# Transposing q and k as 32-bit words that hold two tokens, with kept-back MoE matmuls and a moved lead-in, in an attention and MoE kernel

## The chip, the cores and the metric

The kernel runs on one core of one Trainium2 chip. The metric is the device time of one execution in microseconds (us). Each run carries a state, fast or slow, and only fast runs are compared. The engines are TensorE (PE; its weight loads, which overlap it, are listed as PEld: 270.1 and 141.1 us busy in the kernel before, in a span of 294.5), VectorE (DVE), ScalarE (ACT) and GpSimd (POOL).

## The reference

Causal attention by blocks of 64 tokens over 8 batches of 8 heads, 576 tokens of 64 values, then a mixture layer of two first matmuls, a maximum and an output matmul:

```python
scores = (q @ k.transpose(0, 1, 3, 2)) / np.sqrt(64)      # q, k, v: 8 x 8 x 576 x 64, float32
scores = np.where(block_i >= block_j, scores, -1e9)       # blocks of 64
attn = softmax(scores)
x = (attn @ v).transpose(0, 2, 1, 3).reshape(4608, 512)
out = np.maximum(x @ w1, x @ w2) @ w_out                  # w1, w2: 512 x 1024; w_out: 1024 x 512
```

## The kernel before

The heads go in 32 pairs. A group of two pairs of q (or k) is loaded, cast to bf16 and transposed on PE. For every pair the scores come in two bursts (`burst_a`, `burst_b`) whose exponentials run on ACT; two pairs later the product with v (`av`) is formed in two parts, normalised by DVE (`rec`, `xp`) and transposed into xT (`x_out`). Between these pieces `fill(n)` issues n of the MoE matmuls that are ready: `h` (x times w1 and w2) and `y` (times w_out). Eight of them make a unit.

```python
def cast(nm, g, parts):
    t = raws.pop((nm, g)).rearrange("p s (t d) -> p t s d", d=D)
    qk_n[nm, g] = n = qkn.tile([P, RPP, 2, D], BF16, name=f"{nm}n")        # RPP = 9
    for copy, j0, j1 in parts:
        copy(out=n[:, j0:j1], in_=t[:, j0:j1])

def transposes(nm, g, copies):
    n = qk_n.pop((nm, g))
    pts = [ps_m.tile([P, RPP, NP], BF16, name=f"ps_{nm}T", tag="m") for _ in range(2)]
    for j in range(RPP):
        for i in range(2):                                                 # partitions 0-63, 64-127
            r = slice(i * NP, (i + 1) * NP)
            nc.tensor.transpose(pts[i][:, j, :], n[r, j].rearrange("p s d -> p (s d)"), ident[r, r])
    ...     # DVE or ACT copy pts[i] to qT / kT: out "q (p j) -> q p j", in "q j p -> q p j"

def av(p, ts):
    po = ps_m.tile([P, n, 2, D + 1], FP32, name="ps_o", tag="m")           # the same four buffers
    ...     # 6 matmuls for ts = [0, 1], 24 for [2, 3, 4]; then rec and xp read po

def fill_of(s):
    ...     # 27 for the last two pairs
    left = 10 - s if s < 10 else 4 - (s - 2) % 4
    return -(-ready() // left)
```

The softmax here doesn't subtract the row's maximum and nothing guards it: scores larger than these inputs give would overflow.

## Time and profile before

The three runs before the change have a median of 296.89 us. The run that was profiled took 296.26 us, a span of 294.5. PE is the bound, with 92% busy and 82% of the chain: the prediction below shows its lines. I use one derived figure, the *lag*: the time at which a pair's first score matmul starts, less 0.216 us (the start-to-start time of a settled MoE matmul) for every MoE matmul issued before it. What the lag grows by in a stretch is time that PE gave to anything but MoE matmuls, work or waiting. It is worked out from the instruction records.

| what, kernel before | value |
|---|---|
| lag at the first scores of pair 0 | 8.35 us |
| growth to pair 2, to pair 4 | 7.73, 14.71 |
| growth from pair 4 to 10 (h and y run between, waits for casts) | 15.49 |
| growth 10 to 16, 16 to 28, 28 to 31 | 16.22, 29.99, 7.22 |
| the tail behind pair 31 | 6.39 |
| settled transposes of one group, start to start | 0.27 us |

The rest of the time is the MoE matmuls themselves at 0.216 us each.

### The profile page before, as it was taken

Reading aid. Unit: us, or ns where it says so; the run is one execution under the profiler, and the core shown is the slowest. Engines: PE = TensorE matmul, PEld = TensorE weight load, DVE = VectorE, ACT = ScalarE, POOL = GpSimd, SP = SyncE. Lnnn points to the kernel's source line nnn. Section 1 sums busy time; section 2 is a strip of 40 time slices with the busy share of each in tenths; the row PEclk is TensorE's granted clock in tenths of the full one; section 3 lists DMA queues with packets and bytes.
Section 4 is the critical chain, followed back from the end, with each engine's and each line's share of the span. In section 5 each row is a group of like instructions: output and inputs, shape, how many; then the busy total and the mean of one; then the engine's idle time right before and its main releaser. Section 6 shows DMA issues by size and latency. Waiting matters only on the chain.

```text
span 294.5 us, 7341 instructions
## 1 busy us (share of the span) xinstructions
PE 270.1 (92%) x3033; PEld 141.1 (48%) x3080; DVE 182.6 (62%) x362; ACT 138.4 (47%) x200; POOL 94.4 (32%) x214
## 2 busy tenths in 40 slices
PE   1677989899998999999999999999999999999995
PEld 1245434554554555555554555555544554444443
DVE  6546657647877676666676666667655776464530
ACT  3865557685664555555555555555544000100112
POOL 3955166544632443244324432244210000000000
PEclk9999999999999999999999999999999999999999
DMA  7999997997970639455924792566201011110114
GB/s 270 140 250 314 294 175 119 68 270 247 323 46 2 71 98 183 128 125 103 195 68 168 78 225 41 171 71 75 47 36 44 33 47 60 38 71 36 71 38 143
DMA packets 56082, 36.65 MB, mean 124 GB/s; under 512 B 38769, under 2 KB 43377, under 8 KB 56049
## 3 DMA queue, kind: packets, MB, share of 16 engines
q0 software_dynamic: 41728, 7.87, 33.3%
q1 hardware_dynamic: 13760, 27.60, 27.3%
q10 hardware_dynamic: 560, 0.72, 0.7%
q8 instruction: 24, 0.39, 0.6%
q14 instruction: 10, 0.07, 0.1%
HBM read 34.60 MB, written 9.44 MB: 150 GB/s over the span
## 4 chain that ended last, share of the span: by engine, by line
PE 82%; DVE 8%; ACT 5%; issue 2%; DMA 2%; POOL 1%; POOLq 0%; ACTq 0%; DVEq 0%
PE ps_h L166 41%; PE ps_y L184 19%; PE ps_o L325 10%; PE ps_s L274 7%; ACT aT L280 4%; DVE g L175 2%; PE ps_kT L257 2%; DMA qraw<-in_q_dram 2%; PE ps_qT L257 2%; DVE kT L264 1%; DVE xp L332 1%; PE ps_xe L345 1%; DVE xT L350 1%; DVE xT L351 1%; PE ps_y L201 1%
## 5 line engine op out<-in xcount | busy, mean ns | idle before, releaser
L280 ACT ACTIVATE aT<-ps_s 128x1024 bf16<-128x1024 f32 (+1 forms) x128 | 99.3, 832 | 84.5 <-PE ps_s L274 82.2
L166 PE MATMUL ps_h<-xT,w_sb 128*128 128x512 bf16 x543 | 133.4, 380 | 4.3 <-DVE xT L351 2.6
L166 PEld LDWEIGHTS <-w_sb 128*128 128x128 bf16 x576 | 51.8, 98 | 61.9 <-issue 9.2
L173 DVE CAST h<-ps_h 128x512 bf16<-128x512 f32 x72 | 49.7, 690 | 36.7 <-PE ps_h L166 33.6
L184 PE MATMUL ps_y<-wo_sb,g 128*128 128x512 bf16 x266 | 66.6, 379 | 1.1 <-DVE kT L264 0.3
L285 POOL MEMSET aT<- 64x128 bf16 x128 | 23.4, 201 | 118.2 <-ACT aT L280 118.0
L175 DVE TENSOR_TENSOR g<-h,ps_h 128x512 bf16<-128x512 bf16 x72 | 49.5, 688 | 13.2 <-PE ps_h L166 12.4
L190 ACT COPY y<-ps_y 128x512 f32<-128x512 f32 x35 | 20.6, 588 | 56.9 <-PE ps_y L184 43.7
L325 PE MATMUL ps_o<-vv,aT 128*128 128x65 bf16 x960 | 40.5, 196 | 2.1 <-DVE kT L264 0.6
L325 PEld LDWEIGHTS <-aT 128*128 128x128 bf16 x960 | 35.8, 99 | 13.3 <-issue 3.2
L274 PE MATMUL ps_s<-qT,kT 64*128 64x64 bf16 (+4 forms) x384 | 36.7, 291 | 4.9 <-ACT aT L280 3.3
L184 PEld LDWEIGHTS <-g 128*128 128x128 bf16 x280 | 25.6, 98 | 27.3 <-issue 0.4
L109 POOL DMA_DIRECT2D vv<-in_v_dram x40 | 33.7, 849 | 2.2 <-DMA w_sb<-in_moe_w_dram 2.2
L332 DVE TENSOR_TENSOR xp<-ps_o,rec 128x256 bf16<-128x256 f32 x64 | 31.4, 491 | 2.2
L331 DVE RECIPROCAL rec<-ps_o 128x4 f32<-128x4 f32 x64 | 11.8, 185 | 26.9 <-PE ps_o L325 26.7
L274 PEld LDWEIGHTS <-kT 64*128 64x128 bf16 x384 | 16.9, 97 | 20.6 <-issue 13.7
L264 DVE COPY kT<-ps_kT 128x576 bf16<-128x576 bf16 x17 | 12.8, 756 | 10.4 <-PE ps_kT L257 10.4
L105 POOL CAST qn<-qraw 128x1152 bf16<-128x1152 f32 (+1 forms) x15 | 17.0, 1132 | 5.3 <-DMA qraw<-in_q_dram 4.5
L264 DVE COPY qT<-ps_qT 128x576 bf16<-128x576 bf16 x17 | 12.8, 756 | 7.8 <-PE ps_qT L257 7.7
L105 POOL CAST kn<-kraw 128x1152 bf16<-128x1152 f32 x13 | 14.9, 1147 | 0.8
L257 PE MATMUL ps_qT<-ident,qn 64*128 64x64 bf16 x288 | 7.5, 197 | 6.6 <-DVE qn L105 6.4
L264 ACT COPY qT<-ps_qT 128x576 bf16<-128x576 bf16 x15 | 9.5, 630 | 4.9 <-PE ps_qT L257 4.9
(36 smaller groups left out, 89.7 us busy)
## 6 DMA issues: line engine op xcount, KB each, us to landing
qraw<-in_q_dram SPq DMA_DIRECT2D x16, 576.0 KB, 5.4
out_dram<-y SPq DMA_DIRECT2D x35, 256.0 KB, 2.0
kraw<-in_k_dram SPq DMA_DIRECT2D x15, 576.0 KB, 6.9
vv<-in_v_dram POOLq DMA_DIRECT2D x32, 128.0 KB, 4.5
w_sb<-in_moe_w_dram POOLq DMA_DIRECT2D x4, 256.0 KB, 14.2
w_sb<-in_moe_w_dram POOLq DMA_DIRECT2D x2, 512.0 KB, 23.3
wo_sb<-in_moe_w_out_dram POOLq DMA_DIRECT2D x2, 512.0 KB, 12.6
kraw<-in_k_dram ACTq DMA_DIRECT2D x1, 576.0 KB, 5.4
```

What stands on the lines that cost most here:

```text
L105: copy(out=n[:, j0:j1], in_=t[:, j0:j1])
L109: nc.gpsimd.dma_start(out=vv_r[b % NV][:rows, c, :, :D], in_=v[b, :, c * P:c * P + rows, :].rearrange("h p d -> p h d"),)
L166: nc.tensor.matmul(pt[:], w_sb[:, c, f * P:(f + 1) * P], xT[:, c, t0:t0 + SPAN], start=(c == 0), stop=(c == NDM - 1),)
L173: nc.vector.tensor_copy(out=h1[:], in_=pt[:])
L175: nc.vector.tensor_max(g[:, f, :], h1[:], pt[:])
L184: nc.tensor.matmul(py[:], g[:, f, s * P:(s + 1) * P], wo_sb[:, f, :], start=(f == 0), stop=(f == NFF - 1),)
L264: copies[i](out=t[:, :S].rearrange("q (p j) -> q p j", j=RPP), in_=pts[i].rearrange("q j p -> q p j"),)
L274: nc.tensor.matmul(ps[:m, hh, col:col + w], kT[r, c * P:c * P + m], qT[r, q0:q0 + w], start=True, stop=True,)
L280: nc.scalar.activation(out=aT_r[p % NA][:m, :, a0:a0 + w], in_=ps[:m, :, :w], func=AF.Exp, scale=scale,)
L285: nc.gpsimd.memset(aT_r[p % NA][BLK:, :, a0:a0 + BLK], 0.0)
L325: nc.tensor.matmul(po[:, gi, hh, :], a[:, hh, a0:a0 + P], vv[:, c, h0 + 2 * hh, :], start=(mm == 0), stop=(mm == n_mm - 1),)
L332: nc.vector.tensor_mul(xp[:, ts[0]:ts[0] + n, :, p % 2], po[:, :, :, :D], rec[:, :n].to_broadcast([P, n, 2, D]),)
```

## The change

Its intent is fewer, denser transposes. Two neighbouring tokens' bf16 values are cast side by side into one 32-bit word; the word is transposed as fp32; each PSUM row then holds adjacent bf16 tokens, so the copy out of PSUM reads unit steps. Nine rows are odd, so a tenth, padded one is added. Further: at most all but six of the ready MoE matmuls are spread, so that six are left to cover the wait for xT (`KEEP`); the casts of q and k group 3 go from POOL to DVE and ACT; and in the first four pairs the transposes of k1 and the AV matmuls move.

```diff
-        qk_n[nm, g] = n = qkn.tile([P, RPP, 2, D], BF16, name=f"{nm}n")
+        qk_n[nm, g] = n = qkn.tile([P, RPP // 2 + 1, 2, D, 2], BF16, name=f"{nm}n")
+        to = n.rearrange("p j s d e -> p e j s d")
         for copy, j0, j1 in parts:
-            copy(out=n[:, j0:j1], in_=t[:, j0:j1])
+            for e in range(2):
+                a, z = (j0 - e + 1) // 2, (j1 - e + 1) // 2
+                copy(out=to[:, e, a:z], in_=t[:, 2 * a + e:2 * z + e - 1:2])
...                                     # memsets of the padding for the first six tiles; ident32
-        pts = [ps_m.tile([P, RPP, NP], BF16, ...) for _ in range(2)]
+        pts = [ps_m.tile([P, NP, nj], FP32, ...) for _ in range(2)]        # nj = 5
...
-                    pts[i][:, j, :], n[r, j].rearrange("p s d -> p (s d)"), ident[r, r],
+                    pts[i][:, :, j], n[r, j].rearrange("p s d e -> p (s d e)").bitcast(FP32),
+                    ident32[r, r],
...                                     # the copy out reads the words as bf16 pairs, 9 of 10
+    KEEP = 6
-        return -(-ready() // left)
+        return -(-max(0, ready() - KEEP) // left)
...
-            cast("q", 3, ((pool, 0, RPP),))       # in pool_work(3), behind DMA issues
-            cast("k", 3, ((pool, 0, RPP),))
...
         burst_a(s)                                # pairs 0 to 3
         if s == 0:
             cast("k", 1, ((dve, 0, RPP),))
-        if s >= 2:
-            av(s - 2, [0, 1])
+        elif s == 1:
+            transposes("k", 1, (dve, dve))()
+        elif s == 2:
+            av(0, [0, 1])
+        else:
+            av(0, [2, 3, 4])
         burst_b(s)
...                                     # av(1) follows pair 3, together with av(2) and av(3)
         burst_a(s)                                # pairs 4 to 31
+        if s == HP + 1:
+            cast("q", 3, ((dve, 0, RPP),))
+            cast("k", 3, ((act, 0, RPP),))
```

More of the change, by code (lines that the diff above doesn't have):

```diff
@@ L82 @@
     ident = wpool.tile([P, P], BF16, name="ident")
+    ident32 = wpool.tile([P, P], FP32, name="ident32")
     raws = {}
@@ L102, in cast @@
         t = raws.pop((nm, g)).rearrange("p s (t d) -> p t s d", d=D)
-        qk_n[nm, g] = n = qkn.tile([P, RPP, 2, D], BF16, name=f"{nm}n")
+        qk_n[nm, g] = n = qkn.tile([P, RPP // 2 + 1, 2, D, 2], BF16, name=f"{nm}n")
+        to = n.rearrange("p j s d e -> p e j s d")
         for copy, j0, j1 in parts:
-            copy(out=n[:, j0:j1], in_=t[:, j0:j1])
+            for e in range(2):
+                a, z = (j0 - e + 1) // 2, (j1 - e + 1) // 2
+                copy(out=to[:, e, a:z], in_=t[:, 2 * a + e:2 * z + e - 1:2])
+        if (nm, g) in (("q", 0), ("q", 1), ("q", 2), ("k", 0), ("k", 1), ("k", 2)):
+            nc.vector.memset(n[:, RPP // 2, :, :, 1], 0.0)
     def load_v(b, c):
@@ L133 @@
     make_identity(nc, ident)
+    make_identity(nc, ident32)
     for r in range(NV):
@@ L252, in transposes @@
         n = qk_n.pop((nm, g))
-        pts = [ps_m.tile([P, RPP, NP], BF16, name=f"ps_{nm}T", tag="m") for _ in range(2)]
-        for j in range(RPP):
+        nj = RPP // 2 + 1
+        pts = [ps_m.tile([P, NP, nj], FP32, name=f"ps_{nm}T", tag="m") for _ in range(2)]
+        for j in range(nj):
             for i in range(2):
@@ L265, in copy_out @@
                     out=t[:, :S].rearrange("q (p j) -> q p j", j=RPP),
-                    in_=pts[i].rearrange("q j p -> q p j"),
+                    in_=pts[i].rearrange("q p j -> q (p j)").bitcast(BF16).rearrange(
+                        "q (p j) -> q p j", j=2 * nj)[:, :, :RPP],
                 )
@@ L415 @@
             cast("k", 1, ((dve, 0, RPP),))
-        if s >= 2:
-            av(s - 2, [0, 1])
+        elif s == 1:
[4 more added lines that the diff above has]
+            av(0, [2, 3, 4])
         burst_b(s)
         pool_work(s)
-        if s < 2:
-            transposes("qk"[s], 1, (dve, dve))()
-        else:
-            av(s - 2, [2, 3, 4])
-    for p in (2, 3):
+        if s == 0:
+            transposes("q", 1, (dve, dve))()
+    for p in (1, 2, 3):
         av(p, [0, 1])
         av(p, [2, 3, 4])
-        x_out(p - 2)
+        if p == 2:
+            x_out(0)
+    x_out(1)
     x_due = []
```

## The prediction

> **What bounds the kernel now.** I read the page first, then the groups by shape, the waits of TensorE (PE), the timeline of a settled stretch, and the chain of waits in the first 45 us. Busy time and chain:
>
> ```profile
> PE 270.1 (92%) x3033; PEld 141.1 (48%) x3080; DVE 182.6 (62%) x362; ACT 138.4 (47%) x200; POOL 94.4 (32%) x214
> PE 82%; DVE 8%; ACT 5%; issue 2%; DMA 2%; POOL 1%; POOLq 0%; ACTq 0%; DVEq 0%
> ```
>
> PE is busy 92% of the span and carries 82% of the chain; nobody else is near. The idle 24 us (294.5 - 270.1) lie early: by stretches, PE is busy 16.3 of the first 29 us, 33.1 of 29 to 66, and 126.0 of the 129 us from 91 to 220. What it waits for from 66 to 220 us is short:
>
> ```profile
> PE ps_h L166 <- DVE xT L351: 2.0, 5, 0.6
> PE ps_o L325 <- DVE kT L264: 0.6, 2, 0.3
> PE ps_o L325 <- DVE qT L264: 0.3, 1, 0.3
> ```
>
> The 2.0 us are the five moments when a batch's last x transpose has just been issued and no older MoE matmul is left to run while DVE copies xT.
>
> The transposes concerned, settled (start, duration, engine, operation):
>
> ```profile
> 102.98 0.44 PE L257 MATMUL ps_kT<-ident,kn 64*128 64x64 bf16 x18
> 103.25 0.41 PE L274 MATMUL ps_s<-qT,kT 64*128 64x320 bf16 x6
> ```
>
> Start to start, a group of 18 takes 103.25 - 102.98 = 0.27 us, not the 0.44 that its overlapping records span: 15 ns each, because the two halves (partitions 0-63, 64-127) run side by side. There are 32 groups, so q and k transposes cost PE only 32 x 0.27 = 8.6 us, about 3% of the span. That caps what part one can save.
>
> The evacuation copies, by shape:
>
> ```profile
> L264 DVE COPY qT<-ps_qT 128x576 bf16<-128x576 bf16 x17 | 12.8, 756 | 7.8 <-PE ps_qT L257 7.7
> L350 DVE COPY xT<-ps_xe 128x640 bf16<-128x640 bf16 x16 | 7.8, 486 | 2.6 <-PE ps_xe L345 2.5
> ```
>
> 576 elements read with a step cost 756 ns; 640 read in unit steps, also from PSUM, cost 486.
>
> The early stretch: group 3's casts stand on POOL behind DMA issues that wait, and PE waits for them:
>
> ```profile
> 39.16 1.14 POOL qn L105
> 40.31 1.10 POOL kn L105
> 41.41 0.05 issue
> 41.45 0.62 PE ps_kT L257 x17
> 42.07 0.02 issue
> 42.09 0.77 DVE kT L264
> 42.86 0.04 issue
> 42.90 1.46 PE ps_h L166 x6
> ```
>
> The last h matmul before this stretch has streamed by about 40.0 (it starts at 39.8), the next starts at 42.9; useful PE work between is two transpose groups and six scores, 0.27 + 0.27 + 0.35 = 0.9 us, so 2.0 us are lost.
>
> [...] No fp32 transpose is in this trace. [...] The trace records 98 ns per bf16 load but starts one every 15 ns, so the recorded duration is no pitch; what an fp32 pitch is stays open, and is the largest uncertainty here.[...]
>
> **The change, part by part.** On the instruction lists 576 bf16 transposes (18 a group, each with its own weight load) become 320 fp32 ones (10 a group, no separate weight load listed). Everything else on PE has the same counts.
>
> *Transposes.* A group changes from 0.27 us to t. If an fp32 pair (both halves) streams as one bf16 pair does, t = 10 x 15 ns = 0.15 us: -0.12 x 32 = -3.8 us.[...] The first eight groups (0 to 3) lie where PE waits for other things, so 24 groups count in full: -2.9[...] us. I take 0.30 us[...]: +0.03 x 24 = +0.7 us. I choose nearer the fast end because six padding memsets, a larger tile and retuning were spent around this trick, which only makes sense if it did not cost 20 us; that is an inference about the author and not from the profile.
>
> *Copies.* Source rows become 9 adjacent values of 10[...], what the 640-element xT copy needs: about 490 ns in place of 756. 34 DVE copies save 34 x 0.27 = 9 us of DVE, but DVE is 62% busy: on the path only the 0.9 us of ps_o waits and a few tenths early; -0.5 us. ACT's 627 ns copy[...] I leave it.
>
> *Casts.* One of 1152 becomes 640 + 512 with an output step of two. POOL pays one more fixed cost per cast (estimate: the 1152 cast takes 1149 ns, a 384 one 891 beside DVE; some 0.2 us), about 25 x 0.2 = 5 us on an engine that is 32% busy: off the path. At the very start it adds perhaps 0.2 us before the first scores, with the memsets.
>
> *Moved casts q3, k3* to DVE and ACT: the 2.0 us of waiting above go.
>
> *Moved AV and k1 transpose, first four pairs.* In the chain exp gives way to PE from 14.5 to 16.7 (k1 transpose and its copy) and from 18.7 to 21.0 (24 AV matmuls between score bursts). Moving k1 between the bursts and pushing AV back saves about 0.9 + 1.0 us of that; the DVE normalisations overlap better. My sum is a first h matmul near 26.3 in place of 29.4.
>
> *But the weights.* The six w_sb transfers land at 22.0, 25.2, 29.6, 34.1, 38.1 and 40.6 us (issue time plus time to landing in the DMA view; the last is 16.4 + 24.2), with DMA at 0.9 or more of its time through that stretch. Each h unit of 8 matmuls needs both w halves: h matmul 21 needs the one at 34.1, 33 the one at 38.1, 37 the one at 40.6. Walking the new order (6, q2/k2, 6, scores, 7, scores, 8, scores, 6, q3/k3, scores, 7) from 26.3, matmul 21 would be up at about 33.0 and waits 1.1 us; 37 is up at 40.1 and waits 0.5; matmul 40 ends near 41.5. In the kernel before matmul 41 ends at about 44.3, 40 at 44.1. So the AV part and the cast part, worth 3.1 + 2.0 singly, together give some 2.5 us; the rest becomes a wait for weights.
>
> *Kept-back MoE (six matmuls, 1.3 us)* cover the wait for xT, at most 0.6 us each: -2.0 us from 66 to 220, none from work, as the kept ones are only done later.
>
> Sum: -2.5 - 2.0 - 0.5 + 0.2 + 0.7 = -4.1, on 296.89: 292.8; with the transposes' skew to the fast end I say 292.3.
>
> **Rivals.** *Fp32 weight loads become the bound*[...]. For it: [...]PE has no slack to hide it. Against: row halves overlap in this trace, and weight loads run ahead. *Transposes at 15 ns each and DMA less strict*: -2.9 in place of +0.7 and 1 us more early: 288 us. For it: transfers may also start earlier as buffers come free sooner. Against: DMA is full until 40 us whatever the order. *Early gains hidden wholly by weights or by v of batch 1* (lands by 45.9, while AV of pair 4 would now come near 45): 295 us.
>
> **Range and chances.** Sum at the fast end 288, centre 292[...]. The 2% line is 291.0, so the centre lies just short of it. Range 287 to 302; faster by over 2%: 0.38; within: 0.44; slower: 0.18.
>
> **What would show it.** Start to start of ten fp32 transposes to the following scores: 0.15 to 0.35 us means right[...]. DVE qT copies near 490 ns. No PE wait on xT after 66 us. First h matmul near 26 us, then PE waits on w_sb transfers at 33 to 41 us. What breaks the prediction is the fp32 pitch above all; next, weights landing at other times than before.

## More of the kernel before

All of ps_h, ps_y, ps_o, ps_qT, ps_kT and ps_x share one pool of four PSUM banks (`ps_m`, tag "m"; banks 4 to 7 in the built program). Which of the four a tile gets is fixed when the program is built and depends on the tiles opened and released before it; it is no strict rotation.

## The result, and the profile after

The changed kernel takes 297.53 us (median of 4 runs, 297.23 to 297.60); the kernel before, in the same rounds, 296.95 (296.60 to 297.03). The ratio is 1.002, with a 95% interval of 1.0003 to 1.0037: the same within 2%, if anything slower. Ratios here are the mean time of one kernel's fast runs over that of the other's fast runs of the same rounds, so they are not quite the ratio of the medians quoted. The profiled run (span 295.8) gives the same answer for the bound; PE's busy time has risen in spite of 256 fewer transposes, and its share of the chain too:

```profile
PE 272.8 (92%) x2778; PEld 143.4 (48%) x2824; DVE 177.3 (60%) x373; ACT 142.6 (48%) x205; POOL 103.2 (35%) x240
PE 85%; ACT 5%; DVE 5%; issue 2%; DMA 2%; ACTq 0%
```

The settled transposes in the timeline (start, duration, engine, operation, count):

```profile
101.99 0.53 PE L266 MATMUL ps_kT<-ident,kn 64*128 64x64 f32 x10
...
102.35 0.41 PE L285 MATMUL ps_s<-qT,kT 64*128 64x320 bf16 x6
```

Start to start the ten take 102.35 - 101.99 = 0.36 us, where eighteen took 0.27. In the records of single instructions, the two halves of a pair start within 3 or 4 ns of each other (so they do run side by side), and the pairs follow one another at 62 ns; bf16 pairs follow at 29.

The copies out of PSUM, by shape (busy us, mean ns of one; then idle time before them):

```profile
L361 DVE COPY xT<-ps_xe 128x640 bf16<-128x640 bf16 x16 | 7.8, 490 | 12.4 <-PE ps_xe L356 12.1
L274 DVE COPY kT<-ps_kT 128x576 bf16<-128x576 bf16 x17 | 8.3, 491 | 7.7 <-PE ps_kT L266 7.6
```

They went from 756 to 491 ns, the xT copy's duration, as forecast. The waits of PE from 66 to 220 us hold no xT of h units and no ps_o any more:

```profile
PE ps_h L174 <- issue: 1.4, 9, 0.2
PE ps_y L192 <- DVE xT L361: 0.2, 1, 0.2
```

(The nine short `issue` waits are new; they were not followed up.) So the waits named in the prediction went, and still nothing was won. In the early stretch the wait for group 3 is there, under another name:

```profile
39.00 1.47 PE L174 MATMUL ps_h<-xT,w_sb 128*128 128x512 bf16 x6
40.40 0.53 PE L266 MATMUL ps_qT<-ident,qn 64*128 64x64 f32 x10
42.35 0.53 PE L266 MATMUL ps_kT<-ident,kn 64*128 64x64 f32 x10 [1.43 <-ACT kn L110]
```

and the timeline of ACT says why:

```profile
38.95 1.94 ACT L291 ACTIVATE aT<-ps_s 128x1024 bf16<-128x1024 f32 x2 [1.09 <-PE ps_s L285]
40.78 1.52 ACT L110 CAST kn<-kraw 128x640 bf16<-128x640 f32 x2
```

The k cast was put behind both exponentials of pair 5 in the queue of ACT; it starts at 40.78, as the second of them ends (40.89 by its record), and ends at 42.3. PE's k3 transposes start at 42.35, against 41.45 before: the queue changed and the wait stayed.

Where the time went, by lag growth (us; columns are profiled runs, some from the experiments below; the row "full pace from" says when the clock of PE came to full pace, which the next section takes up):

| stretch | before | after | words_again | keep_only | lead_only | keep8 | after_keep8 | lead_keep8 |
|---|---|---|---|---|---|---|---|---|
| full pace from, us | 22.5 | 24.7 | 27.2 | 27.6 | 22.8 | 27.8 | 24.3 | 23.3 |
| to first scores | 8.35 | 9.19 | 9.17 | 8.15 | 8.29 | 8.28 | 8.86 | 8.36 |
| pair 0 to 2 | 7.73 | 7.11 | 7.57 | 7.74 | 7.11 | 7.73 | 7.11 | 7.11 |
| 2 to 4 | 14.71 | 15.12 | 15.70 | 15.86 | 14.80 | 15.85 | 15.12 | 14.96 |
| 4 to 6 | 4.42 | 4.62 | 3.78 | 3.86 | 4.53 | 3.86 | 4.62 | 5.37 |
| 6 to 10 | 11.07 | 11.75 | 11.07 | 11.80 | 11.07 | 11.93 | 11.91 | 11.93 |
| 10 to 16 | 16.22 | 15.16 | 15.68 | 15.04 | 16.22 | 15.45 | 15.07 | 15.46 |
| 16 to 28 | 29.99 | 30.69 | 31.05 | 31.13 | 29.99 | 29.51 | 30.14 | 29.51 |
| 28 to 31 | 7.22 | 7.19 | 7.40 | 7.26 | 7.23 | 6.99 | 7.10 | 7.00 |
| tail | 6.39 | 6.62 | 6.39 | 6.61 | 6.38 | 6.38 | 6.39 | 6.39 |

Before to after, the rows differ by +0.84, -0.62, +0.41, +0.20, +0.68, -1.06, +0.70, -0.03 and +0.23, which sum to 1.35, the difference of the spans (1.3). There is no single hole; there are gains of 1.7 us and losses of 3.1. Of the 0.41 in 2 to 4 some 0.3 goes with the later moment of full pace: lead_only, with the same order and full pace from 22.8 us, has 14.80 there. The medians differ by 0.6 us and not by 1.3, because the profile before is one of the quicker runs of its kernel.

### The profile page after: what moved, and what is told of

Read it like the earlier page. It is cut to its first block, busy times and chain, and to the rows that moved or that the text cites. A ratio compares the mean times of both kernels' runs of the same rounds, so it can differ in the third digit from the quotient of the medians.

```text
span 295.8 us, 6882 instructions
## 1 busy us (share of the span) xinstructions
PE 272.8 (92%) x2778; PEld 143.4 (48%) x2824; DVE 177.3 (60%) x373; ACT 142.6 (48%) x205; POOL 103.2 (35%) x240
## 3 DMA queue, kind: packets, MB, share of 16 engines
q1 hardware_dynamic: 13760, 27.60, 27.2%
## 4 chain that ended last, share of the span: by engine, by line
PE 85%; ACT 5%; DVE 5%; issue 2%; DMA 2%; ACTq 0%
PE ps_h L174 41%; PE ps_y L192 18%; PE ps_o L336 11%; PE ps_s L285 8%; ACT aT L291 4%; PE ps_kT L266 2%; DVE xp L343 2%; PE ps_qT L266 2%; DMA qraw<-in_q_dram 2%; PE ps_xe L356 2%; DVE rec L342 1%; PE ps_y L209 1%; ACT kn L110 0%; DVE xT L361 0%; DVE qn L110 0%
## 5 line engine op out<-in xcount | busy, mean ns | idle before, releaser
L174 PE MATMUL ps_h<-xT,w_sb 128*128 128x512 bf16 x556 | 135.9, 379 | 2.8 <-issue 1.6
L291 ACT ACTIVATE aT<-ps_s 128x1024 bf16<-128x1024 f32 (+1 forms) x128 | 99.3, 832 | 56.6 <-PE ps_s L285 51.9
L192 PE MATMUL ps_y<-wo_sb,g 128*128 128x512 bf16 x254 | 64.6, 379 | 1.0 <-DVE xT L361 0.2
L183 DVE TENSOR_TENSOR g<-h,ps_h 128x512 bf16<-128x512 bf16 x72 | 49.3, 684 | 10.1 <-PE ps_h L174 9.7
L336 PE MATMUL ps_o<-vv,aT 128*128 128x65 bf16 x960 | 41.2, 197 | 1.7 <-DVE xp L343 0.6
L336 PEld LDWEIGHTS <-aT 128*128 128x128 bf16 x960 | 35.0, 100 | 13.9 <-DVE xp L343 7.0
L192 PEld LDWEIGHTS <-g 128*128 128x128 bf16 x280 | 25.5, 98 | 27.2 <-issue 0.6
L285 PEld LDWEIGHTS <-kT 64*128 64x128 bf16 x384 | 18.0, 98 | 20.3 <-issue 13.9
L110 POOL CAST qn<-qraw 128x640 bf16<-128x640 f32 (+3 forms) x28 | 21.5, 815 | 4.8 <-DMA qraw<-in_q_dram 4.1
L110 POOL CAST kn<-kraw 128x640 bf16<-128x640 f32 (+1 forms) x24 | 18.9, 834 | 0.8
L266 PE MATMUL ps_qT<-ident,qn 64*128 64x64 f32 x160 | 9.0, 243 | 7.0 <-DVE qn L112 7.0
L361 DVE COPY xT<-ps_xe 128x640 bf16<-128x640 bf16 x16 | 7.8, 490 | 12.4 <-PE ps_xe L356 12.1
L266 PEld LDWEIGHTS ps_qT<-ident,qn 64*128 64x128 f32 x160 | 6.7, 148 | 13.0 <-POOL qn L110 7.4
L274 DVE COPY kT<-ps_kT 128x576 bf16<-128x576 bf16 x17 | 8.3, 491 | 7.7 <-PE ps_kT L266 7.6
```

The source lines that it names most:

```text
L110: copy(out=to[:, e, a:z], in_=t[:, 2 * a + e:2 * z + e - 1:2])
L174: nc.tensor.matmul(pt[:], w_sb[:, c, f * P:(f + 1) * P], xT[:, c, t0:t0 + SPAN], start=(c == 0), stop=(c == NDM - 1),)
L183: nc.vector.tensor_max(g[:, f, :], h1[:], pt[:])
L192: nc.tensor.matmul(py[:], g[:, f, s * P:(s + 1) * P], wo_sb[:, f, :], start=(f == 0), stop=(f == NFF - 1),)
L266: nc.tensor.transpose(pts[i][:, :, j], n[r, j].rearrange("p s d e -> p (s d e)").bitcast(FP32), ident32[r, r],)
L285: nc.tensor.matmul(ps[:m, hh, col:col + w], kT[r, c * P:c * P + m], qT[r, q0:q0 + w], start=True, stop=True,)
```

## The experiments

My theory after the result: the parts don't fail together but one by one; the words cost PE more than the copies return, KEEP loses what it gains, the moved casts change a name only, and the moved lead pays. The rival: one of them (the fp32 transposes, the visible change in PE's work) ate gains that the others do have.

**words_only**: the word layout, ident32 and the fp32 transposes alone, in the kernel before (the first three hunks of the diff).

> The kernel before with the 32-bit words alone (new cast layout, fp32 transposes, padding memsets), no KEEP, old order of casts and AV. Theory A (the words are the loser): a settled group of transposes takes 0.36 us as in the changed kernel, not 0.27, so 28 groups on a full PE cost 28 x 0.09 = 2.5 us, and the start 0.5 to 0.8 us more: 299.5 to 300.5 us. Rival B (the words pay through the faster DVE copies, and something else lost): 296 to 297 us. Both expect DVE qT copies of 490 ns.

Measured: 297.50 us, ratio 1.0013 (0.9993 to 1.0033), timed over 5 rounds. The profile fell into a slow execution (468.7 us, mean clock 0.58) and is not used; the same kernel ran again for its trace.

**words_again**: the same kernel, one look.

> The same kernel as words_only, whose one profile fell in a slow execution: wanted is a profile in the fast state. Theory A: from pair 16 to pair 28 (12 settled pairs, one transposes group each) it takes 12 x 0.09 = 1.1 us more than the kernel before, and DVE's faster copies give back less than 0.3 us of it. Rival B: no more than 0.3 us longer, as the copies pay.

Measured: 297.94 us, one run, state unknown, its mean clock 1.0. Read by its trace, 16 to 28 grew by 31.05 against 29.99: +1.06, or 0.09 us in each of the 12 pairs, just what one group of transposes a pair costs. From 10 to 16 the lag is 0.54 us *lower*: there the shorter DVE copies took away the waits of PE on qT and kT (0.9 us from 67 to 96 us before, none here; those on xT stayed). The start is 0.82 us later. By the ratio the words thus cost about what I had forecast for them in sum (+0.4 us), by terms that were each several times as large.

**keep_only**: KEEP = 6 alone.

```diff
+    KEEP = 6
-        return -(-ready() // left)
+        return -(-max(0, ready() - KEEP) // left)
```

> The kernel before with KEEP = 6 alone. Theory A: the 2.0 to 2.6 us of PE waits on the xT copy go and nothing takes their place: 294.3 to 295 us. Rival B: the wait turns up elsewhere (on DVE's g and copies behind it): 296.5 to 297 us. In both no PE wait on xT over 0.2 us is left after 60 us.

Measured: 297.65 us, ratio 1.0027 (1.0004 to 1.0050): slower, where I had forecast a gain of 2.0 us. PE no longer waits for xT between 66 and 220 us, and its busy time there is the whole of both windows that I read (25.00 of 25 us, 129.00 of 129). Yet 16 to 28 grows by 1.14 more than before. A full busy row and a longer time need a look at the weight loads; their waits, 95 to 215 us, kernel keep_only:

```profile
PEld L325 <- DVE xp L332: 7.2, 16, 0.5
```

That is the load of the second AV part waiting for the normalisation (`xp`) of the first, once in each of 16 pairs. Its timeline, keep_only:

```profile
149.40 0.59 PE L184 MATMUL ps_y<-wo_sb,g 128*128 128x512 bf16 x2
149.47 0.42 DVE L332 TENSOR_TENSOR xp<-ps_o,rec 128x256 bf16<-128x256 f32 x1
...
149.95 0.91 PE L325 MATMUL ps_o<-vv,aT 128*128 128x65 bf16 x24
```

and the same place in the kernel before:

```profile
149.95 0.81 PE L184 MATMUL ps_y<-wo_sb,g 128*128 128x512 bf16 x3
150.27 0.42 DVE L332 TENSOR_TENSOR xp<-ps_o,rec 128x256 bf16<-128x256 f32 x1
...
150.59 0.90 PE L325 MATMUL ps_o<-vv,aT 128*128 128x65 bf16 x24
```

Before, three y matmuls take 150.59 - 149.95 = 0.64 us, which is 3 x 0.216, and AV starts while xp is still being written (it ends at 150.69). In keep_only two take 149.95 - 149.40 = 0.55 in place of 0.43, and AV starts only after xp has ended at 149.89. The bank numbers in the built program say what the wait is (no trace shows them; building the kernels again gave the same): in the kernel before, the two AV parts of a pair never stand in the same one of the four banks in this stretch; with KEEP = 6 they do for 16 pairs, during the scores of pairs 14 to 29. My reading is that six kept matmuls are not a whole unit of eight, so another tile is open where the parts take theirs; the next run tests whether the shared bank is what costs. The loss is hidden from the busy row by the records: a MoE matmul is recorded for 379 ns but gives way to the next after 216, so a gap of up to 0.16 us is covered by its tail.

**keep8**: eight, a whole unit, in place of six.

```diff
+    KEEP = 8
```

> The kernel before with KEEP = 8: a whole h unit kept back, with which, by the bank numbers in the built program, no pair's two AV parts share a PSUM buffer (with 6, 16 pairs do). Theory A (the shared buffer is what 6 loses by): from pair 16 to 28 it takes 29.1 us beyond its MoE matmuls as keep24 did (before 30.0, keep_only 31.1), and less is held back from the first batch than with 24: 295.3 to 296.2 us, ratio 0.994 to 0.997. Rival B (any holding back costs as much early as it saves later): ratio 0.998 or more.

Measured: 296.05 us, ratio 0.9969 (0.9956 to 0.9982). No pair shares a bank, by the built program; 16 to 28 is 29.51, 1.62 below keep_only and 0.48 below before. So by these ratios KEEP is worth 0.9 us if its number keeps the two parts in different banks, and costs 0.8 if not.

**keep24**: many kept, to see how far it goes.

```diff
+    KEEP = 24
```

> The kernel before with KEEP = 24 in place of 6: one whole cycle of 8 h, 8 y, 8 h matmuls, so no h pair of tiles is left half done when the transposes ask for PSUM buffers. Theory A (the six kept ones shift the cycle so that both AV parts of a pair fall on one PSUM buffer and the second waits 0.16 us for DVE): xT waits gone and no new waits, from pair 16 to 28 some 1.3 us less than keep_only, time 294.5 to 295.5 us. Rival B (keeping matmuls back costs in itself, the work only moves to the end): 296.7 to 297.7 us as keep_only.

Measured: 296.66 us, ratio 0.9984 (0.9959 to 1.0008), no clear difference. 16 to 28 fell to 29.08, the lowest of all, but 6 to 10 grew to 12.73 from 11.07: with the first batch's matmuls held back PE waited for exponentials there (1.9 us in four waits from 44 to 66 us, where the kernel before has none). What is kept back is missing where it would have filled.

**lead_only**: the moved k1 transposes and AV alone.

> The kernel before with the moved AV and k1 transposes alone. Theory A: the exps of pairs 0 to 3 run closer (scores of pair 3 start about 1.4 us earlier), but PE then[...] reaches its fast pace (30 in place of 55 ns per AV matmul) about 2 us later, and the normalisations on DVE that must follow start no earlier: first h matmul within 0.5 us of before (29.4), time 296.5 to 297.5 us. Rival B (my prediction's): first h matmul at 27 us or sooner, 294.5 to 295.5 us.

Measured: 295.83 us, ratio 0.9963 (0.9943 to 0.9984). The first four h matmuls without a gap begin at 28.84 us, 0.59 before the 29.43 of the kernel before, and not 3.1 before:

```profile
28.84 1.02 PE L166 MATMUL ps_h<-xT,w_sb 128*128 128x512 bf16 x4 [0.38 <-DVE xT L351]
```

From the first scores of pair 0 to those of pair 3 it gained 1.30 us (10.67 against 11.97), and from there to pair 4, where the postponed AV of pair 1 now stands, 0.77 was given back. Neither theory was right: full pace came at 22.8 us, not late as A had it, and the first h not near B's 27.

**casts_only**: the casts of q3 and k3 moved alone, as in the last hunk.

> The kernel before with the q3, k3 casts moved to DVE and ACT alone. Theory A: the k3 cast stands in ACT's queue behind both exps of pair 5, so it ends near 41.5 us as on POOL (41.4): the wait for it is kept and only changes its name, 296.6 to 297.2 us. Rival B (my prediction's): the 2.0 us of waiting go, 294.7 to 295.3 us.

Measured: 297.48 us, ratio 1.0009 (0.9986 to 1.0032). The 2.0 us of waiting that I had counted did not go: PE now waits 0.93 us for the k cast on ACT, and later for the copy behind it.

**casts_early**: the same casts, but both on DVE and one pair sooner.

```diff
-        if s == HP + 1:
-            cast("q", 3, ((dve, 0, RPP),))
-            cast("k", 3, ((act, 0, RPP),))
+        if s == HP:
+            cast("q", 3, ((dve, 0, RPP),))
+            cast("k", 3, ((dve, 0, RPP),))
```

> The kernel before with the q3, k3 casts both on DVE and one pair earlier (pair 4) than in the change. Theory A (in the change they stood behind ACT's exps, so the wait only changed its name): the transposes of group 3 no longer wait for a cast, PE is not idle from 40 to 42.9 us, gain 0.6 to 1.5 us, less than the 2.0 idle as the last weights land at 40.6: ratio 0.995 to 0.998. Rival B (the weights take the place of the cast wholly): ratio 0.999 to 1.001, with PE waiting on a w_sb transfer.

Measured: 296.38 us, ratio 0.9982 (0.9963 to 1.0000). 4 to 6 shrank by only 0.26 us. The casts are ready at once, and then PE waits for the copies: 0.8 us on qT of DVE before the k transposes, 0.6 on kT after them. The wait for group 3 is a chain of cast, transposes and copies with buffers between them; one link shortened makes the next one visible.

**The clock.** The runs of the kernel before fall in two heaps: of its 43 fast runs beside the experiments, 6 took 295.88 to 296.17 us, 3 lay between, and 34 took 296.80 or more. The traces hold records of PE's granted clock, which the page's clock row (9 in every slice) doesn't resolve. PE begins at about half pace (no grant is on record yet; in the kernel before, AV matmuls start 54 ns apart before 22.5 us and 29 after) and is given full pace once: at 22.5 us in the profile before and at 22.2 in casts_early, where 2 to 4 grew by 14.71; at 26.9 to 27.8 in words_again, keep_only, keep8, keep24 and casts_only, where it grew by 15.70 to 15.86. So about 1.05 us belong to the moment of the grant in the order of the kernel before, and the profile that I predicted from was one of the early ones. The pace is visible in durations, kernel after:

```profile
20.82 1.50 PE L336 MATMUL ps_o<-vv,aT 128*128 128x65 bf16 x24
...
26.80 0.91 PE L336 MATMUL ps_o<-vv,aT 128*128 128x65 bf16 x24 [0.26 <-DVE xp L343]
...
30.09 1.02 PE L174 MATMUL ps_h<-xT,w_sb 128*128 128x512 bf16 x4 [0.59 <-DVE xT L362]
```

The same 24 matmuls take 1.50 us before the grant at 24.7 and 0.91 after it. That raised a question: is the early stretch slow because PE is at half pace?

**warm_start**: ten matmuls of 512 columns on memset data from 1.5 us on, while PE would wait for q.

```diff
+    dm = ring.tile([P, 512], BF16, name="dm")             # filled by a DVE memset
+    def busy(n):
+        pt = ps_m.tile([P, 512], FP32, name="ps_d", tag="m")
+        for _ in range(n):
+            nc.tensor.matmul(pt[:], dm[:, :P], dm[:], start=True, stop=True)
+    busy(10)
     cq = transposes("q", 0, (dve, act))
```

> The kernel before with ten 512-column matmuls on a constant tile in front of the first transposes, while PE would wait for q. Theory A (PE runs at half pace, 55 in place of 30 ns per AV matmul,[...] and the moment differs between executions, from 22 to 27 us): full pace from about 7 us, first h matmul 1 to 2.5 us sooner than 29.4, time 294.5 to 296 us, and a smaller spread. Rival B[...]: pace as before, 296.7 to 297.3 us.

Measured: 297.22 us, ratio 1.0008 (0.9990 to 1.0025). Full pace was granted at 6.7 us, taken back at 10.1 and given again at 27.1. Six score matmuls of 512 columns take 0.61 us at 8.51 and 1.03 at 11.85. Here a start alone didn't hold it.

**hot**: such matmuls also between the score bursts, two to four at a time, to hold it.

```diff
         burst_a(s)
+        busy(3)
...
         burst_b(s)
+        busy(2)
```

> The kernel before with warm_start's ten matmuls and some more between the score bursts of the first four pairs, results unread. In warm_start the clock records show full pace granted at 6.7 us and taken back at 10.1 until 27.1. Theory A (early PE load too light): full pace holds from 7 us, first h matmul at 27 to 28.5 us, ratio 0.990 to 0.995. Rival B: the clock drops again, ratio 1.000 to 1.004 as the extra matmuls delay the scores.

Measured: 296.74 us, ratio 0.9999 (0.9977 to 1.0021). Full pace stood from 6.5 us to the end (the 24 AV matmuls at 19.92 us take 0.89 us). The first scores came 0.8 us later, and the first h without a gap at 30.05 against 29.43. From first scores to that h it is 20.88 us at full pace and 21.08 in the early-granted kernel before (21.89 in warm_start, granted late). So before some 22 us PE's pace made no more than those 0.20 us here (from 8 to 30 us the chain of the kernel before is 40% exponentials on ACT and 25% DVE); the grant between 22 and 27 us made 0.8. So this cheap remedy, which I would have recommended, brought nothing in this form (the extra matmuls also delayed the first scores).

**bench**: the changed kernel with a series of bare transposes appended, 16 pairs of each kind, at full pace.

```diff
+    bench([(BF16, ident, 64, 128, 64), (FP32, ident32, 64, 128, 64),      # type, identity, rows, weights, moving
+           (FP32, ident32, 32, 128, 32), (FP32, ident32, 64, 64, 64), (BF16, ident, 64, 128, 64)])
```

> The changed kernel with, at its end, 32 transposes of each of five kinds whose results nobody reads: bf16 64x128 on 64 columns, fp32 the same, fp32 with 32 moving columns, fp32 with 64 stationary columns, bf16 again. Outputs right, time longer by some 5 us. Theory A (the weight load sets the fp32 pitch): per pair 29, 62, 62, about 35, 29 ns. Rival B[...]: 29, 62, about 35, 62, 29 ns.

Measured (one run, 302.13 us, state unknown, correct; the series is extra work): bf16 pairs follow at 29 ns, fp32 pairs at 63, fp32 with 32 rows and 32 moving columns at 62, fp32 with 64 weight columns at 56, bf16 again at 29. Neither the weight load nor the stream, my two explanations, holds alone: halving the stream (and the rows) changed the pitch by 1 ns, halving the weights by 7; both at once were not run. What sets some 60 ns for an fp32 pair stays open. In the records the load of a pair starts only as the matmul of the pair before starts, and its own matmul follows some 56 ns later; with bf16 the order is the same, and the matmul follows 27 ns after its load. That is a description and not a cause.

**best**: the moved lead, KEEP = 8 and the early casts together, with bf16 transposes.

> The kernel before with bf16 transposes kept, AV and k1 moved as in the change, KEEP = 8, and both group-3 casts on DVE at pair 4. If the parts add: -1.1 us (lead_only) - 1.3 (keep8) - 0.9 (casts_early) = 293.7 us, ratio 0.986 to 0.991. If what one part frees early is lost to the weights that land at 40.6: 295 us, ratio 0.992 to 0.995.

Measured: 297.64 us, ratio 1.0022 (1.0000 to 1.0044), worse than each of its parts. 6 to 8 grew by 9.25 in place of 5.44. PE's waits from 44 to 60 us, first line of that view, and the timeline there:

```profile
PE ps_o L325 <- DMA vv<-in_v_dram: 1.3, 2, 0.8
```

```profile
48.50 0.98 PE L325 MATMUL ps_o<-vv,aT 128*128 128x65 bf16 x15 [0.52 <-DMA vv<-in_v_dram]
49.70 2.34 PE L166 MATMUL ps_h<-xT,w_sb 128*128 128x512 bf16 x5 [0.22 <-issue]
```

PE had come to batch 1 before its v had landed, the third rival of the prediction. And it came at a price beyond the wait: the five h matmuls behind it have 2.34 us, where five take 1.24 in the kernel before, and the clock records show half pace from 48.5 to 51.9. Four of the six runs of best have a mean clock of 0.994, and these took 297.3 to 298.6 us; the other two took 296.4 and 297.2. A stretch of 3.4 us at half pace takes 0.5 x 3.4 / 295 = 0.6% off the mean clock, so the mean clock of a run tells of such an event. (The kernel before has a few such runs too, of 296.9 to 298.4 us.)

The accounts of the parts were taken on the kernel before. What was left open was whether they hold inside the changed kernel, and whether a better sum exists.

**no_words**: the changed kernel without the words: bf16 transposes; KEEP = 6, the moved casts and the moved lead stay.

> The changed kernel with bf16 transposes and the old casts (ident32 and the word layout taken out; KEEP = 6 and the moved casts and AV stay). Theory A (the fp32 transposes cost 0.09 us in each of the 28 groups from pair 4 on, less what the shorter DVE copies give back to the shared-bank waits): 16 to 28 about the same as in keep_only (31.1, the bank wait comes back at its long size), start 0.8 us earlier than after, start-to-pair-0 at 8.3, 10 to 16 near 15.0; about 296.5 us, 1 us below after and within 0.3% of before. Theory B (the words are neutral in this company, what they cost on PE comes back through DVE): 297.5 as after.

Inconclusive. The profile fell into a slow execution (552 us) and can't be used; the five fast runs are 296.99, 297.50, 298.44, 300.04 and 300.69, the last two with a mean clock of 0.994; ratio 1.0068 (1.0030 to 1.0106). Neither theory forecast such a spread. The two slowest have the mark of the half-pace event that best showed, but no trace of them was taken, so what lies behind it stays open. The one experiment that takes the words out of the changed kernel thus says nothing.

**after_keep8**: the changed kernel with KEEP = 8.

```diff
-    KEEP = 6
+    KEEP = 8
```

> The changed kernel with KEEP = 8 in place of 6; no pair's two AV parts share a PSUM bank any more (17 of 32 in after). Theory A (the shared bank is a loss in the changed kernel too): no waits of AV on xp of their own pair, stretch 16 to 28 falls from 30.7 to about 30.0 to 30.5 (bf16 keep8 had 29.5, plus 12 x 0.09 us of transposes), 296.6 us. Theory B (with DVE copies of 490 ns the shared bank costs nothing): 16 to 28 stays at 30.7 and the time within 0.3 us of after, 297.5.

Measured: 296.49 us median; five runs of 295.77 to 296.72 and one of 299.45 with a mean clock of 0.994, which makes the ratio 1.0004 with a wide interval (0.9972 to 1.0036). The trace bears out theory A: no wait of AV on the xp of its own pair, and 16 to 28 at 30.14, down 0.55 from the changed kernel's 30.69. What remains above keep8's 29.51 is 0.63, of the 12 x 0.09 = 1.1 us that slow transposes cost there; some of it comes back, as it did in words_again. By medians across rounds KEEP = 8 in place of 6 is worth about 1 us of the changed kernel, 0.55 of it seen in 16 to 28; by the ratio, with the one disturbed run in, that isn't settled.

**lead_keep8**: the two parts that pay, with bf16 transposes and the old casts.

> The kernel before with the moved AV and k1 transpose and KEEP = 8; casts and transposes as before. Theory A (the parts add when batch 1's v is not hurried: lead -1.1, keep8 -0.9): pair 0 to 2 at 6.2, 16 to 28 at 29.5, 28 to 31 at 7.0, pair 6 to 8 below 6.5; 295.0 us, ratio 0.993. Theory B (the lost time in run best came from lead and KEEP = 8 together): 6 to 8 again above 8 us, a wait of PE on v of batch 1 and half pace of the clock around 50 us; 296.5 to 297.5.

Measured: 295.56 us (295.18 to 296.44), ratio 0.9962 (0.9944 to 0.9980); the kernel before in these rounds 296.88. It is the best median of all and beats both kernels, by 0.4% and, across rounds, by 0.7%. By the ratios the parts don't add: -1.1 and -0.9 make -1.1. In the profile, the rows from 6 on are those of keep8 and row 0 to 2 is that of lead_only, 7.11 (the 6.2 of the forecast was my slip: I had counted to the last scores of pair 1). What is missing is in 4 to 6, 5.37 against 4.53 and 3.86. The timelines of PE and POOL there, lead_keep8:

```profile
38.01 1.47 PE L166 MATMUL ps_h<-xT,w_sb 128*128 128x512 bf16 x6
40.94 0.44 PE L257 MATMUL ps_qT<-ident,qn 64*128 64x64 bf16 x18 [1.46 <-POOL qn L105]
...
39.73 1.14 POOL L105 CAST qn<-qraw 128x1152 bf16<-128x1152 f32 x1
```

and lead_only:

```profile
37.90 1.68 PE L166 MATMUL ps_h<-xT,w_sb 128*128 128x512 bf16 x7
39.87 0.44 PE L257 MATMUL ps_qT<-ident,qn 64*128 64x64 bf16 x18 [0.29 <-POOL qn L105]
...
38.67 1.14 POOL L105 CAST qn<-qraw 128x1152 bf16<-128x1152 f32 x1
```

PE is through with its h matmuls at about the same time (38.01 + 6 x 0.216 = 39.31 and 37.90 + 7 x 0.216 = 39.41), but POOL casts q of group 3 1.06 us later here. It stands behind a DMA issue that waits for the fifth w_sb transfer, which landed at 38.67 us in this run and at 37.60 in lead_only; in the other fast profiles it lands between 37.4 and 38.5. So the loss in this row is largely the landing time of one run. That run took 296.20 us, the second slowest of the six, and three of the others 295.18 to 295.26; whether the parts add in the quicker ones stays open. A's rows are there except this one, and B's wait for v and half pace are not in the trace (one of the six runs has 0.994).

## Why the prediction was right or wrong

The time lay in the range (287 to 302), but the centre, 292.3, was 5.2 us low and I had the change down as a gain. The singles, by ratio on 297 us, are +0.4 (words), +0.8 (KEEP), -1.1 (lead) and +0.3 (casts), which sum to +0.4; the changed kernel measured +0.6 (interval +0.1 to +1.1). With some 0.6 us of uncertainty in each of the four, that agreement is no proof, and by rows the parts don't add: from 10 to 28 the words alone gave -0.54 + 1.06 and KEEP alone -1.18 + 1.14, together +0.48, and the changed kernel has -0.36. What falls is the rival that the transposes alone ate the gains, for KEEP = 6 and the moved casts show no gain to be eaten even with bf16 transposes. Of the steps below, KEEP, the moved casts and the moved lead failed, and the transposes were mis-sized.

*What bounds it*: right. PE stayed the bound in every profile that was not slow (76 to 88% of the chain).

*Transposes, "I take 0.30 us"*: a size, and an estimate of mine with no measured fp32 transpose behind it. The group measures 0.36, so +0.09 in each of the 28 groups from pair 4 on, +2.5 us and not +0.7. The direction and the working side by side were right (the halves of a pair start 3 or 4 ns apart); the fast end, 0.15, which I leaned to for the author's effort, was not. An inference about why someone made a change is no measurement. Nor is an instruction list a trace: I had read "no separate weight load" there, and the trace has one for each fp32 transpose (320, of 139 ns in the median).

*Copies, "-0.5 us"*: the duration was right (491; I had taken the about 490 from the 486 of the 640-element xT copy). Their gain on the path was under-counted: in 10 to 31 words_again lost 0.7 us (-0.54 + 1.06 + 0.18), where 20 groups at 0.09 would be 1.8. So the copies gave back about 1.1 there. In 4 to 10, where 6 groups cost 0.5, the lag fell by 0.64; part of that is PE coming later to the casts of group 3 (warm_start, unchanged there, fell by 0.26).

*Casts, "perhaps 0.2 us before the first scores"*: 0.84. I had costed them by instructions and not by shape. Kernel before, then after:

```profile
5.76 0.56 DVE L105 CAST qn<-qraw 128x768 bf16<-128x768 f32 x1 [0.31 <-DMA qraw<-in_q_dram]
```

```profile
5.86 1.04 DVE L110 CAST qn<-qraw 128x384 bf16<-128x384 f32 x2 [0.41 <-DMA qraw<-in_q_dram]
```

One cast of 560 ns became two of 577, each of half its elements. By shape, kernel after:

```profile
L110 DVE CAST qn<-qraw 128x640 bf16<-128x640 f32 x1 | 0.9, 875 | 0.0
...
L110 DVE CAST qn<-qraw 128x512 bf16<-128x512 f32 x1 | 0.5, 486 | 0.0
```

640 elements are five rows, 512 are four, 384 are three, and the 768 before were six. From the two odd row counts of qn, an element takes (875 - 577) / 256 = 1.16 ns and the fixed part is 130; with the same fixed part the even counts take (486 - 130) / 512 = 0.70 and (560 - 130) / 768 = 0.56 ns. So the odd ones run at about half the pace. The kernel before agrees, without the words: its one cast of nine rows on DVE takes (1352 - 130) / 1152 = 1.06 ns an element.

```profile
L105 DVE CAST kn<-kraw 128x1152 bf16<-128x1152 f32 x1 | 1.4, 1352 | 0.6 <-DMA kraw<-in_k_dram 0.6
```

One kind of row does not fit: the first k cast on DVE is slow with an even count too (four rows, 726 ns before; two rows, 703 after, where the second cast of two rows takes 293). So the odd count is a likely reason, not tested by itself.

*Moved casts, "the 2.0 us of waiting above go"*: failed. I asked when the new engine has time and not what stands in its queue. k3's cast stood behind two exponentials on ACT, and where it didn't (casts_early) PE waited for the next link.

*Moved AV, "a first h matmul near 26.3"*: failed in size. Alone it is 28.84 where the kernel before has 29.43, and in the changed kernel 30.09, as the slow start (+0.84) and a later grant of full pace came on top. I had subtracted moved AV work from the front without adding it where it went: the AV of pair 1 stands between pairs 3 and 4 and takes back 0.77 of 1.30 us there, and behind it one chain of DVE operations leads to the first xT. Two profiles with early full pace (22.8 and 22.5 us) differ by 0.5 us of span, so this is what the order itself is worth in them. The rest of lead_only's 1.1 us may be that its order gets full pace early more often (five of its six runs lie at 295.7 to 295.9, one at 296.85); only profiled runs show the grant, so I leave that open.

*"But the weights"*: the landings were right within 1.5 us (22.0, 23.8, 28.3, 32.7, 38.5, 41.2 after), but no PE wait on w_sb appeared, because h was never early enough to meet them. A correct limit on a gain that did not come.

*KEEP, "-2.0 us from 66 to 220, none from work"*: the step that failed most. Alone it gave -1.18 in 10 to 16, +1.14 in 16 to 28 and +0.04 in 28 to 31 (67 to 223 us), so 0.0 in place of -2.0, and over the whole kernel +0.8 by the ratio (its profile shows +0.2 outside 2 to 4, where the grant of full pace lies). The xT waits went as forecast. But which bank a tile gets depends on how many tiles were opened before it, and six kept matmuls moved this so that the second AV part waits for the normalisation of the first. The sum from 6 to 10 also rose by 0.7, for want of filler as keep24 suggests. I had called it a change of order and free.

*Range and rivals*: the fp32 rival named the right place (+0.09 us a group), though halving the weights took only 7 of 63 ns off a pair in bench; the rival of v was not seen in the changed kernel and was in best. That the time of the kernel before has two heaps 1 us apart was in none of the steps. I had used a profile of the lower one.

## What to carry to other kernels

Follow a change of issue order through the buffers: work out which bank or buffer each tile gets before and after, and hold back an amount that leaves them in different banks (here 8 and 24 did, with 29.51 and 29.08 from 16 to 28, and 6 did not, with 31.13). Where an engine is busy all the time and the kernel is slower, compare start-to-start times with the settled pitch and read the waits of the weight loads, as records longer than the pitch (here 379 ns against 216) hide gaps. A wait that sits at the end of a chain (cast, transposes, copy) wasn't removed here by moving one link (0.26 us of the 2.0 in casts_early); and gains early in a kernel can end at the next thing that arrives by its own schedule, as in best at the v of batch 1 (waits of 0.82 and 0.52 us), so they need not add.
